# The first weight load of a decode block, split into 16 and 112 partitions, with other row distances in DRAM

## The chip, the cores and the metric

The kernel runs on one core of one Trainium2 chip. The metric is the time of one execution on the device, in microseconds. Several executions are timed, and their median counts. One execution more is recorded by the hardware profiler; the trace and the profile come from that one.

A core has these engines: PE multiplies matrices, DVE and ACT work on vectors, POOL is the general engine, and SP does nothing here but issue transfers. Sixteen DMA engines move the data between DRAM and the on-chip memory, which has 128 partitions. A transfer that SP or ACT issues is cut into packets, which the DMA engines take up.

## What is computed

One decode step of a transformer block, for eight sequences with one token each, all in float32. With `D = 1024`, 32 query heads, 4 key/value heads of width 128, the last 1,024 positions of the cache, and a hidden width of 3,584, the reference comes down to this:

```
q  = layernorm(x) @ wq                       # 1024 x 4096
p  = softmax(q . k_cache[last 1024] * 128**-0.5)
h  = x + (p . v_cache[last 1024]) @ wo       # 4096 x 1024
n  = layernorm(h)
out = h + (gelu(n @ w_gate) * (n @ w_up)) @ w_down   # 3584 wide
```

Every weight and every cache entry is read once and used for eight tokens only. That makes 111 MB to be loaded for one step.

## The kernel before, in words

The weights and the two caches are laid out on the host as twelve units of 128 rows by 16,384 elements, which is 65,536 bytes a row and 8 MiB a unit. In their order these are two units each for `wq`, the keys, the values and `wo`, and four for the gate and up projections with a part of the down projection. The last rows of the down projection follow in smaller arrays: `dn` (three loads), `tails` (two) and `ends` (two).

On the chip there are two buffers, `wbuf[0]` and `wbuf[1]` (L110, L111), for one unit each. Row p of a unit goes to partition p. The units alternate between the buffers, so that one is filled while PE works on the other.

The loop at L150 issues the twelve loads, all from SP and so on one queue, by way of the helper `move` (L91), which starts a transfer and lets it add 16 to a semaphore when it has landed. Unit 0 and unit 1 are issued at once. Each later unit waits until PE has finished with the unit two places before it (`free`, L152). The load of `x`, eight rows of 4,096 bytes to partitions 0, 4, ... 28, is issued from ACT behind the first unit (L155) and lies on a queue of its own.

DVE computes the layer norm of `x` (L247), PE turns the result by eight transposes (L240), and DVE copies it twice into the stationary operands `still[0]` and `still[1]` (`spread`, L271, the copy in L274). Each of these copies adds 1 to `go[0]` or `go[1]`. PE then runs passes of 64 multiplications over one buffer (`half`, L214, the multiplication in L222). Ahead of a pass it waits until that buffer's semaphore `go[i]` has 17: 16 from the load and 1 from the stationary operand (L232, L243). It takes the 17 off again, and so the same semaphore serves the next unit in that buffer.

After the first two passes come the scores, the softmax, the values, the output projection, the second layer norm and the gated projections in the same pattern. DVE and ACT prepare the next stationary operand while PE works on the other buffer. At the end the last rows of `down` are multiplied (L428, L454), added up (L457) and stored in two transfers, one from SP and one from ACT.

The function `kernel` (L484) prepares the arrays on the host. L517 joins the twelve units to one array, in which all rows lie back to back.

Of the kernel before, what the change touches and what calls it, by code (L numbers as in the profile page):

```python
# [7 lines left out]
P = 128  # L8
B = 8
D = 1024  # L10
# [4 lines left out]
NC = D // P  # L15
NQ = 4
# [3 lines left out]
BUF = NC * SET  # L20
# [10 lines left out]
ENDPARTS = (2, 1)  # L31
ENDS = (160, 96)
AHEAD = 3


GATE = (1, 16, 16)
# [5 lines left out]
class Flow:  # L42
# [37 lines left out]
    def run(self, engine, make, *waits, mark=True, gives=None):  # L80
        ins = self.start(engine, make, waits)
        if gives is not None:
            ins.then_inc(*gives)
            return None
        if not mark:
            return None
        self.done[engine] += 1
        ins.then_inc(self.own[engine], 1)
        return self.own[engine], self.done[engine]

    def move(self, name, out, src, *waits, engine="sync", sem=None):  # L91
        s = self.sem(name) if sem is None else sem
        self.start(engine, lambda e: e.dma_start(out, src), waits).then_inc(s, 16)  # L93
        return s, 16


def decode_block(nc, x, units, dn, tails, ends, outs):

    fl = Flow(nc)
    run, move = fl.run, fl.move  # L100
# [3 lines left out]
    def sb(name, *shape):  # L104
        return nc.alloc_sbuf_tensor(name, list(shape), F32).ap()
# [5 lines left out]
    wbuf = [space[:, i * BUF:(i + 1) * BUF] for i in range(2)]  # L111
# [6 lines left out]
    go = [fl.sem("go_a"), fl.sem("go_b")]  # L118
# [4 lines left out]
    at_mark = {}  # L123
# [26 lines left out]
    for u in range(UNITS):  # L150
        k, i = divmod(u, 2)
        free = None if k == 0 else (half_a, half_b)[i](k - 1)  # L152
        move(f"u{u}", wbuf[i], units[u], free, sem=go[i])
        if u == 0:
            x_in = move("x", x_sb[0:ROWS:STEP, :], x, x_zero, engine="scalar")  # L155

# [19 lines left out]
    for i, (n, src) in enumerate(zip(ENDS, ends)):  # L176
        t = wbuf[1][:, c0:c0 + NQ * n]
# [20 lines left out]
    own = sb("own", P, HB)  # L198
# [48 lines left out]
    def layernorm(src, ready, name, room):  # L247

        bn = sb(name + "_bn", ROWS, D // N, 6)
        tok = None  # L250
        for i in range(D // N):
            tok = run("vector", lambda e, i=i: e.bn_stats(bn[:, i], src[:, i * N:(i + 1) * N]), ready)
        mv, ve, sd, r0, r1, r2, rs = (
            sb(f"{name}_{n}", ROWS, k) for n, k in
            (("mv", 2), ("ve", 1), ("sd", 1), ("r0", 1), ("r1", 1), ("r2", 1), ("rs", 1))
        )
        tok = run("vector", lambda e: e.bn_aggr(mv, bn), tok)
        tok = run("vector", lambda e: e.tensor_scalar(ve, mv[:, 1:2], EPS, None, op0=ALU.add), tok)
        tok = run("scalar", lambda e: e.activation(sd, ve, AF.Sqrt), tok)
        tok = run("vector", lambda e: e.reciprocal(r0, sd), tok)  # L260

        tok = run("vector", lambda e: e.scalar_tensor_tensor(
            r1, r0, r0, ve, op0=ALU.mult, op1=ALU.mult), tok)
        tok = run("vector", lambda e: e.tensor_scalar(
            r2, r1, -0.5, 1.5, op0=ALU.mult, op1=ALU.add), tok)
        tok = run("vector", lambda e: e.tensor_mul(rs, r0, r2), tok)
        run("vector", lambda e: e.tensor_scalar(
            source[0:ROWS], src, mv[:, 0:1], rs, op0=ALU.subtract, op1=ALU.mult), tok, room,
            gives=(go_turn, 1))

    def spread(k):  # L271

        for i in range(2):
            run("vector", lambda e: e.tensor_copy(  # L274
                still[i].rearrange("p (c j m) -> p c j m", c=NC, j=NQ),
                turned.rearrange("p (c m) -> p c m", c=NC)[:, :, 0:32].unsqueeze(2).to_broadcast(
                    [P, NC, NQ, 32])), at_mark["t", k], gives=(go[i], 1))


    layernorm(x_sb, x_in, "ln1", src_ok)  # L280
    spread(0)


    side_by_side = [source[:, hf * N:(hf + 1) * N] for hf in range(2)]
# [12 lines left out]
    for hf in range(2):  # L297
# [3 lines left out]
        for s in range(2):  # L301
            for a in range(2):
                for b in range(HB):
# [6 lines left out]
                        gives=(go[hf], 1) if end else None)  # L310
# [3 lines left out]
    for hf in range(2):  # L314
# [7 lines left out]
        if hf == 1:  # L322
            run("vector", lambda e: e.tensor_copy(still[0], turned), at_mark["t", 2], half_a(1),
                gives=(go[0], 1))
# [4 lines left out]
        gives=(go[1], 1))  # L329


    for hf in range(2):
# [3 lines left out]
        for h in range(2):  # L336
            o3 = sums[hf][:, h * N:(h + 1) * N].rearrange("p (b d) -> p b d", b=HB)
            for b in range(HB):
# [5 lines left out]
                else:  # L344
# [3 lines left out]
                        gives=(go_turn, 1) if end and hf else None)  # L348
        cleared[hf] = run("gpsimd", lambda e: e.memset(still[hf], 0.0), done(2))  # L349

    for hf in range(2):
# [12 lines left out]
        gives=(go_fold, 1))  # L364
    h_sb = sb("h_sb", ROWS, D)
    h_ok = run("vector", lambda e: e.tensor_add(h_sb, x_sb, turned[0:ROWS]), at_mark["y", 3])
    layernorm(h_sb, h_ok, "ln2", None)
    run("gpsimd", lambda e: e.memset(note[:, 7:8], 0.0), at_mark["t", 5], gives=(go_fold, 2))
    spread(5)
    rest = sb("rest", P, N)  # L370
    for ch in range(2):
# [8 lines left out]
    for k, n in enumerate(SETS):  # L380
# [5 lines left out]
        if k == 1:  # L386
# [9 lines left out]
            gives=(go_turn, 1))  # L396
        t = turned[:, 0:N].rearrange("p (i m) -> p i m", m=P)
# [9 lines left out]
        else:  # L407
# [3 lines left out]
                at_ok, gives=(go_later[0], 1))  # L411
# [33 lines left out]

    ahead = sb("ahead", 1, AHEAD)
    for i in range(AHEAD):
        run("vector", lambda e: e.memset(ahead[:, i:i + 1], 0.0), arrived[last - 1][1], d1_ok)
# [110 lines left out]
```

## Time and profile before

| | |
|---|---|
| median of three runs | 263.96 us (263.74 to 263.99) |
| profiled execution | 263.65 us |
| its span, from the first to the last instruction | 262.3 us |
| mean granted clock of PE | 0.798 |
| PE, DVE, ACT, POOL busy | 140.4, 43.8, 13.5, 7.2 us |
| bytes read from DRAM | 111.18 MB |
| mean rate over the span | 424 GB/s |
| DMA packets | 3040 |

The profiled execution is timed like the others, and its span is the part between the first and the last instruction. In the views, "busy" is the time in which an engine worked on an instruction. Idle time is put down to what ended it, for example "<-PE sum L222" for a wait that ended with PE's multiplication into `sum` in line 222. The DMA rows give the share of the sixteen DMA engines' time that packets filled, and the rate in GB/s; a packet counts for the window in which it starts. For a transfer, the time to landing runs from its issue to the end of its last packet, and so it holds the time in the queue behind earlier transfers.

### The profile page before, as it was taken

Reading aid. Unit: us, or ns where it says so; the run is one execution under the profiler, and the core shown is the slowest. Engines: PE = TensorE matmul, PEld = TensorE weight load, DVE = VectorE, ACT = ScalarE, POOL = GpSimd, SP = SyncE. Lnnn points to the kernel's source line nnn. Section 1 sums busy time; section 2 is a strip of 40 time slices with the busy share of each in tenths; the row PEclk is TensorE's granted clock in tenths of the full one; section 3 lists DMA queues with packets and bytes.
Section 4 is the critical chain, followed back from the end, with each engine's and each line's share of the span. In section 5 each row is a group of like instructions: output and inputs, shape, how many; then the busy total and the mean of one; then the engine's idle time right before and its main releaser. Section 6 shows DMA issues by size and latency. Waiting matters only on the chain. (4 is left out here: it accounts for less than half of the span.)

```text
span 262.3 us, 2253 instructions
## 1 busy us (share of the span) xinstructions
PE 140.4 (54%) x968; PEld 44.4 (17%) x968; DVE 43.8 (17%) x115; ACT 13.5 (5%) x19; POOL 7.2 (3%) x18
## 2 busy tenths in 40 slices
PE   0025705926806937607918408728509709309985
PEld 0021201211202322102302102122102202002321
DVE  0340200240100140400410100254100300100332
ACT  1000000000030010000000200000300000200000
POOL 5000100100000000100100000000000000000000
PEclk9999975985966965975976956965977957956999
DMA  8998997999899799989979998997999999799896
GB/s 320 485 420 380 480 480 320 480 480 420 380 480 480 320 480 480 430 370 480 480 320 480 480 420 380 480 480 320 480 480 410 390 480 480 320 432 487 367 422 230
DMA packets 3040, 111.31 MB, mean 424 GB/s; under 512 B 472, under 2 KB 728, under 8 KB 992
## 3 DMA queue, kind: packets, MB, share of 16 engines
q1 hardware_dynamic: 2880, 111.23, 98.4%
q10 hardware_dynamic: 160, 0.08, 0.1%
HBM read 111.18 MB, written 0.13 MB: 424 GB/s over the span
## 5 line engine op out<-in xcount | busy, mean ns | idle before, releaser
L222 PE MATMUL sum<-w,still 128*32 128x512 f32 x832 | 116.1, 719 | 96.9 <-PEq L209 96.9
L222 PEld LDWEIGHTS sum<-w,still 128*32 128x32 f32 x832 | 31.9, 129 | 176.9 <-issue 176.9
L240 PE MATMUL turned<-ident,source 128*128 128x128 f32 x64 | 11.1, 331 | 21.0 <-PEq L209 21.0
L240 PEld LDWEIGHTS turned<-ident,source 128*128 128x128 f32 x64 | 8.9, 170 | 26.3 <-issue 26.3
L235 PE MATMUL turned<-y_sb,add 128*32 128x512 f32 x24 | 11.3, 592 | 0.9 <-PEq L209 0.9
L318 DVE TENSOR_REDUCE nmax<-sum 128x1 f32<-128x1024 f32 x2 | 2.5, 1225 | 28.4 <-PE sum L222 28.4
L393 DVE TENSOR_TENSOR up<-up,sum 128x512 f32<-128x512 f32 (+1 forms) x2 | 1.4, 686 | 34.2 <-PE sum L222 34.2
L289 DVE TENSOR_SCALAR q<-sum 128x512 f32<-128x512 f32 x2 | 1.4, 692 | 25.1 <-PE sum L222 25.1
L274 DVE COPY still<-turned 128x1024 f32<-128x1024 f32 x4 | 4.7, 1220 | 4.2 <-PE turned L240 4.2
L383 DVE TENSOR_TENSOR gate<-gate,sum 128x512 f32<-128x512 f32 (+1 forms) x2 | 1.4, 684 | 23.6 <-PE sum L222 23.6
L345 DVE SCALAR_TENSOR_TENSOR o<-sum,share,o 128x128 f32<-128x128 f32 x12 | 4.2, 351 | 4.2 <-PE sum L222 3.8
L342 DVE TENSOR_SCALAR o<-sum,share 128x128 f32<-128x128 f32 x2 | 0.7, 351 | 23.9 <-PE sum L222 23.9
L320 ACT ACT_TABLE_LOAD x1 | 1.3, 1283 | 60.1 <-DVE nmax L318 60.1
L235 PEld LDWEIGHTS turned<-y_sb,add 128*32 128x32 f32 x24 | 2.6, 110 | 8.7 <-issue 8.7
L349 POOL MEMSET still<- 128x1024 f32 x2 | 1.9, 952 | 76.0 <-PE sum L222 76.0
L362 DVE TENSOR_TENSOR y_sb<-y_sb,sum 128x512 f32<-128x512 f32 x1 | 0.7, 689 | 15.8 <-PE sum L222 15.8
L360 ACT COPY y_sb<-sum 128x512 f32<-128x512 f32 x1 | 0.6, 586 | 50.7 <-PE sum L222 50.7
L294 POOL MEMSET still<- 128x1024 f32 x2 | 1.9, 958 | 46.3 <-PE sum L222 46.3
L320 ACT ACTIVATE source<-sum,nmax 128x1024 f32<-128x1024 f32 x2 | 2.2, 1115 | 17.1 <-PE turned L240 17.1
L361 DVE TENSOR_TENSOR y_sb<-y_sb,sum 128x512 f32<-128x512 f32 x1 | 0.7, 689 | 14.3 <-PE sum L222 14.3
L305 DVE COPY still<-turned 128x16 f32<-128x16 f32 x32 | 2.7, 161 | 2.1 <-PE turned L240 2.1
L382 ACT COPY gate<-sum 128x512 f32<-128x512 f32 (+1 forms) x2 | 1.2, 584 | 30.3 <-PE sum L222 30.3
(61 smaller groups left out, 40.2 us busy)
## 6 DMA issues: line engine op xcount, KB each, us to landing
w<-dn SPq DMA_DIRECT2D x1, 5120.0 KB, 22.2
w<-dn SPq DMA_DIRECT2D x1, 2048.0 KB, 26.7
w<-dn SPq DMA_DIRECT2D x1, 1024.0 KB, 28.7
w<-tails SPq DMA_DIRECT2D x1, 1024.0 KB, 12.2
w<-tails SPq DMA_DIRECT2D x1, 512.0 KB, 13.1
w<-ends SPq DMA_DIRECT2D x1, 320.0 KB, 13.4
w<-units SPq DMA_DIRECT2D x12, 29.4
w<-ends SPq DMA_DIRECT2D x1, 192.0 KB, 13.4
```

What stands on the lines that cost most here:

```text
L222: ins = PE.matmul(sums[i][32 * j:32 * j + 32, h * N:(h + 1) * N], still[i][:, 32 * s:32 * s + 32], wbuf[i][:, s * N:(s + 1) * N], start=(c ...
L235: ins = PE.matmul(turned[0:32, ch * N:(ch + 1) * N], add2[:, ch, :], y_sb, start=True, stop=True)
L240: ins = PE.transpose(turned[:, n * P:(n + 1) * P], source[:, n * P:(n + 1) * P], ident)
L274: run("vector", lambda e: e.tensor_copy(still[i].rearrange("p (c j m) -> p c j m", c=NC, j=NQ), turned.rearrange("p (c m) -> p c m", c=NC) ...
L289: tok = run("vector", lambda e: e.tensor_scalar(q_sb, sums[hf][:, 0:N], scale, None, op0=ALU.mult), done(0, 0))
L294: cleared.append(run("gpsimd", lambda e: e.memset(still[hf], 0.0), done(0)))
L305: run("vector", lambda e: e.tensor_copy(to[:, :, b, s, a, REP * b:REP * b + REP].rearrange("p k (h i) -> p k h i", h=2), frm[:, s, a * HB ...
L318: tok = run("vector", lambda e: e.tensor_reduce(out=nmax, in_=sums[hf], axis=AX.X, op=ALU.max, negate=True), done(1))
L320: p_ok = run("scalar", lambda e: e.activation(source, sums[hf], AF.Exp, bias=nmax, accum_out=tot), tok, at_mark["t", 1 + hf])
L345: tok = run("vector", lambda e: e.scalar_tensor_tensor(out, o3[:, b], share[hf][:, b:b + 1], o_sb, op0=ALU.mult, op1=ALU.add), tok, done(2 ...
L349: cleared[hf] = run("gpsimd", lambda e: e.memset(still[hf], 0.0), done(2))
L383: tok = run("vector", lambda e: e.tensor_add(gate[:rows], gate[:rows], sums[0][:rows, N:2 * N]), tok, half_a(4 + k))
```

## The change

Three constants are added. `FIRST = 16` is the number of partitions of a new, separate first load. `GAP = 18880` elements, 75,520 bytes, is the distance of the rows of the second load. `PAD = 128` elements, 512 bytes, lie unused behind each row of the other eleven units.

The first unit is kept in two arrays of its own. `head` has rows 0 to 15, in rows of 7 x 18,880 elements, that is 528,640 bytes apart. `body` has rows 16 to 127, 75,520 bytes apart. Sixteen times seven rows of `body` begin at the same distances from one another as the sixteen rows of `head`. The rows of the other units are 66,048 bytes apart.

The load of unit 0 becomes two, issued one after the other from SP. The first fills partitions 0 to 15 and has a semaphore of its own, `first`. The second fills partitions 16 to 127 and adds to `go[0]` as before. So PE's wait for 17 covers the second load alone. The first is waited for by DVE: `spread(0, first)` puts the wait on the copies into the stationary operands, and without their increments PE does not start. What is computed, the order of the other loads and all multiplications stay.

```diff
+PAD = 128
+FIRST = 16
+GAP = 18880
...
-        move(f"u{u}", wbuf[i], units[u], free, sem=go[i])
+        if u == 0:
+            first = move("first", wbuf[i][0:FIRST], head[:, 0:BUF])
+            move("u0", wbuf[i][FIRST:P], body[:, 0:BUF], sem=go[i])
+        else:
+            move(f"u{u}", wbuf[i], units[u - 1][:, 0:BUF], free, sem=go[i])
...
-    def spread(k):
+    def spread(k, *waits):
 
         for i in range(2):
             run("vector", lambda e: e.tensor_copy(
                 still[i].rearrange("p (c j m) -> p c j m", c=NC, j=NQ),
                 turned.rearrange("p (c m) -> p c m", c=NC)[:, :, 0:32].unsqueeze(2).to_broadcast(
-                    [P, NC, NQ, 32])), at_mark["t", k], gives=(go[i], 1))
+                    [P, NC, NQ, 32])), at_mark["t", k], *waits, gives=(go[i], 1))
...
-    spread(0)
+    spread(0, first)
...
+    head = np.pad(units[0, 0:FIRST], ((0, 0), (0, (P // FIRST - 1) * GAP - BUF)))
+    body = np.pad(units[0, FIRST:P], ((0, 0), (0, GAP - BUF)))
+    units = np.pad(units[1:], ((0, 0), (0, 0), (0, PAD)))
```

More of the change, by code (lines that the diff above doesn't have):

```diff
@@ L94, in move, with decode_block @@
         return s, 16
-def decode_block(nc, x, units, dn, tails, ends, outs):
+def decode_block(nc, x, head, body, units, dn, tails, ends, outs):
     fl = Flow(nc)
@@ L531 @@
     arrays = {
-        "x": own(A_x).reshape(B, D), "units": own(units), "dn": dn, "tails": tails, "ends": ends,
+        "x": own(A_x).reshape(B, D), "head": own(head), "body": own(body), "units": own(units), "dn": dn, "tails": tails, "ends": ends,
     }
```

## The prediction

> **What bounds the kernel now.** I read the page first for its 40 slices and DMA queues, then the chain that ended last, the waits of the DMA-issuing queue, and last the DMA answers for short windows at the start.
>
> ```profile
> span 262.3 us, 2253 instructions
> ...
> PE 140.4 (54%) x968; PEld 44.4 (17%) x968; DVE 43.8 (17%) x115; ACT 13.5 (5%) x19; POOL 7.2 (3%) x18
> ...
> DMA  8998997999899799989979998997999999799896
> ...
> q1 hardware_dynamic: 2880, 111.23, 98.4%
> ```
>
> Queue q1 (SP's loads) carries 111.23 MB, and its packets fill 98.4% of the time of all sixteen DMA engines. The busiest compute engine, PE, is busy 54%. No slice of the DMA row stands at zero: the engines never run dry between the first load and the last.
>
> ```profile
> SPq L93 <- PE sum L222: 238.9, 12, 29.7
> ```
>
> ```profile
> w<-units SPq DMA_DIRECT2D x12, 29.4
> ```
>
> SP does wait for PE (238.9 us in 12 waits, for a buffer to come free), but that is no loss: a weight unit lands 29.4 us after its issue, and the next rows show that the transfer itself takes 19.4, so each load stands some 10 us in the queue behind its predecessor. Whatever makes the engines deliver earlier moves the whole program earlier; a PE step made shorter would not.
>
> ```profile
> core 0: us, PE busy (x) PEld busy (x) DVE busy (x) ACT busy (x) POOL busy (x), PEclk, DMA share, GB/s
> ...
> 100.00:119.36 19.36, 9.09 (x64) 2.50 (x64) 2.81 (x8) 0.00 (x0) 0.95 (x1) 0.76 1.00 433
> ```
>
> In the steady state 433 GB/s for 19.36 us are 8.4 MB, one unit of 128 rows of 65,536 bytes, at a DMA share of 1.00. Sixteen engines, eight rows each: 2.42 us a row, 27.1 GB/s an engine. PE needs 9.09 of these 19.36 us.
>
> ```profile
> DMA packets 16, 1.05 MB, mean 524 GB/s; under 512 B 0, under 2 KB 0, under 8 KB 0
> ...
> q1 hardware_dynamic: 16, 1.05, 152.9%
> ```
>
> ```profile
> DMA packets 16, 1.05 MB, mean 419 GB/s; under 512 B 0, under 2 KB 0, under 8 KB 0
> ...
> q1 hardware_dynamic: 16, 1.05, 96.7%
> ```
>
> These are the DMA answers for 1 to 3 us and for 4 to 6.5 us. A packet is credited to the window in which it starts, so a share can pass 100%. Each window holds exactly one row per engine. The first: 152.9% of 2 us on 16 engines is 48.9 us, 3.06 us a row. The second: 96.7% of 2.5 us on 16 engines is 38.7, 2.42 us a row. So every engine loses 0.64 us on its first row and, by the steady window above, nothing after it.
>
> ```profile
> 1.70:1.80 0.10, 0.00 (x0) 0.00 (x0) 0.00 (x0) 0.00 (x0) 0.10 (x1) 1.00 9.77 3277
> 1.80:2.00 0.20, 0.00 (x0) 0.00 (x0) 0.00 (x0) 0.00 (x0) 0.12 (x2) 1.00 5.90 1966
> 2.00:2.20 0.20, 0.00 (x0) 0.00 (x0) 0.00 (x0) 0.00 (x0) 0.20 (x2) 1.00 2.77 983
> 2.20:2.40 0.20, 0.00 (x0) 0.00 (x0) 0.18 (x1) 0.00 (x0) 0.20 (x1) 1.00 1.73 655
> ```
>
> ```profile
> 0.74 0.85 SPq L93 DMA_DIRECT2D w<-units  x2
> ```
>
> GB/s times width over 65,536 bytes gives how many engines start in each stretch: 5, 6, 3 and 2. The start is a ramp of some 0.6 us that begins 1.0 us after the issue at 0.74. The last two starters need 1.73 x 0.2 x 16 / 2 = 2.77 us for their row, less than the 3.06 of all.
>
> **The change part by part.** The sum is made against the profiled execution: 263.65 us, of which 262.3 are span and 1.35 lie around it. It stands 0.31 below the median of 263.96.
>
> *Row pitch and gaps in DRAM.* No byte more is read; the unused bytes are stepped over. In the steady state there is nothing to win on the rows shown, since the engines are full at 2.42 us a row with the present pitch of 65,536 bytes. Whether another pitch could lose is bounded by the first load of down-projection rows, 40,960 bytes long and apart, which fills this answer for 236 to 247 us:
>
> ```profile
> DMA packets 138, 4.80 MB, mean 436 GB/s; under 512 B 13, under 2 KB 13, under 8 KB 13
> ...
> q1 hardware_dynamic: 138, 4.80, 101.2%
> ```
>
> 436 GB/s at 101.2% is the same pace per engine. I take 0 for units 1 to 11. At the start, sixteen engines set out nearly together, at distances that are whole multiples of 65,536 bytes; if that is why they lose 0.64 us, the new distances cure it. Bounds: 0 (another cause) to -0.64 (all of it). I take -0.5, between the 0.29 that the last two starters already gain (3.06 - 2.77) and 0.64, nearer to the latter, since at 528,640 bytes no two of the sixteen are a multiple of 65,536 apart, while the last two starters still were.
>
> [...]
>
> *Two loads in place of one.* The first load now has one row per engine, the second seven. If the ramp is the time in which 128 rows are handed out, it shrinks to an eighth; if it is per engine, nothing changes. Bounds: 0 to -0.6 for the last starter. I take -0.3, half, because the mean engine starts only some 0.2 us behind the first. The seven remaining rows are issued one SP instruction later; such an instruction takes 328 to 426 ns here:
>
> ```profile
> L93 SPq DMA_DIRECT2D w<-units x12: 328/328/426, 0.7 to 205.4; - x12
> ```
>
> So they are issued by 1.2 us, and 1.0 to 1.6 us later (the row at 0.74 and the ramp) the engines have them: 2.2 to 2.8. The first rows are done at about 1.75 + 2.5 = 4.2. That cover is 1.4 us; were it gone, the engines would stand for what is missing. Unit 1 is issued 0.4 us later and needed at about 21: 0. One more completion per engine: a unit of 8 rows with its completion takes 19.36 against 8 x 2.42 = 19.36, below 0.02.
>
> *The added wait.* DVE's first expansion of the stationary operand (L274) also waits for `first`. Queued behind it on DVE is the second expansion, and PE's first multiplication waits for both:
>
> ```profile
> 16.15 2.36 DVE L274 COPY still<-turned 128x1024 f32<-128x1024 f32 x2 [2.12 <-PE turned L240]
> ```
>
> ```profile
> 22.68 8.54 PE L222 MATMUL sum<-w,still 128*32 128x512 f32 x64 [6.57 <-PEq L209]
> ```
>
> DVE comes to it at 16.15, some 12 us after `first` should be there, and PE starts at 22.68, 4.2 us after DVE's end at 18.51. Cost 0. If the weights come 0.8 earlier, 3.4 of that slack is left. Next in line after the start is again the DMA stream itself; the end is untouched.
>
> *Sum:* -0.5 - 0.3 = -0.8; 262.85 in the profile's terms, 263.2 as a median.
>
> **The rivals.**
>
> *Slower: neighbouring partitions share their way into the on-chip memory.* `first` sends all sixteen engines to partitions 0 to 15. If a way takes no more than one engine delivers, 27.1 GB/s, the steady window needs sixteen ways for a load over 128 partitions; at sixteen one way serves up to eight partitions, and sixteen neighbours have between two and sixteen ways: one to eight engines share one. With two sharing, the first row takes 2 x 2.42 = 4.84, 1.8 more than the 3.06 of now; with four 9.68, +6.6; with eight 19.4, +16.3. It decides from two engines on a way. I price it at the middle case, four: 263.96 + 6.6 = 270.6. The seven rows of the second load, if engine after engine takes seven neighbours, would meet in pairs now and then: 0 to 7 x 2.42 = 16.9 more. For it: no row of the trace has a bulk load on fewer than 128 partitions, so nothing shows that the ways are free to choose. Against it: nothing in the trace shows such sharing either.
>
> The Trainium skill ("SBUF — State Buffer", Door 1: The DMA port swizzle) states that partitions 0-15 reach four of sixteen ports and gives 104 GB/s measured there for 1 MiB. That is just the size of `first`: by that page an estimated 10.1 us for it, 7.0 more than now, and a time near 271. No run here shows it.
>
> *No change: a cold start.* The 0.64 us is what any first row costs, whatever its address, and the ramp belongs to the engines. Then the pitches do nothing and splitting at most 0.3: 263.7 to 264.0. For it: the second rows, started with the same spread of 0.6 us, lose nothing, though their distances are the same. Against it: the last two starters lose 0.35 where the mean loses 0.64, and a fixed price would be equal for all.
>
> *The rows are not dealt out evenly.* If 112 rows go to fourteen engines, eight each, these have nine rows in all: 2.42 - 0.8 = 1.6 more, 265.6. Against it: 112 divides by sixteen.
>
> **How the numbers follow.** Forecast 0.47, sharing 0.29, cold start 0.20, uneven 0.04. What a measurement of this kernel can tell from no change is about 0.2%, 0.53 us. The forecast's own range is 262.7 (263.96 - 0.64 - 0.6) to 263.6; a tenth of it lies within 0.53 of now. Faster: 0.43. Same: 0.20 and 0.04, 0.24. Slower: 0.29 and 0.04, 0.33. The range for 8 in 10 must take in part of the sharing: from 262.7 up to 273.5, that is +6.6 and about 3 us of pairing in the second load; beyond it are some 0.15, and below it 0.03.
>
> **What would show it.** Right: the answer for the first microseconds has sixteen packets of 65,536 bytes at about 2.5 us each, started within 0.1 to 0.2 us; unit 0 lands, and PE's first multiplication starts, 0.8 us earlier (about 21.9); the steady window still has 433 GB/s. Sharing: the first sixteen packets take 5 to 10 us each, and PE starts at 24 or later, at about 29 with four on a way. Cold start: 3.06 us a row again, PE at 22.4 or later. The forecast is wrong, too, if the pitch of the other units changes the steady 2.42 us a row, which would count 88 times per engine.

## The result, and the profile after

The changed kernel takes 285.45 us (median of 6 runs, 285.26 to 285.8) against 263.91 (263.74 to 264.04) for the kernel before: slower by 21.5 us, ratio 1.0819 with a 95% interval of 1.0808 to 1.0831. I had forecast 263.2 and a range up to 273.5. The likeliest case was wrong in sign, and the rival that has the right cause was priced too low.

The page of the changed kernel shows at once that the loss lies at the start:

```profile
span 283.9 us, 2255 instructions
...
DMA  9799799989999999999999989999999999989994
GB/s 148 148 300 268 175 277 415 425 388 415 443 443 443 443 425 443 443 443 443 443 434 434 425 379 425 434 443 443 443 434 434 443 443 443 443 389 415 410 411 184
...
q1 hardware_dynamic: 2896, 111.23, 98.2%
```

The DMA engines are as busy as before (98.2% after 98.4), and the bytes are the same. But "busy" here means that a packet is under way, not that it moves: in the first six slices, 43 us, the rate is 148 to 300 GB/s, and from then on it is about 430 GB/s, as before. A busy share without the rate beside it would have hidden the whole loss.

The next rows are the windows of the changed kernel, laid around the successive rows of unit 0; the row at 40.50 is the first of unit 1, and the last one a steady stretch. The last two columns are the share of the DMA engines and GB/s; wherever width times GB/s is 1.05 MB, there are sixteen rows in it, and share times width is the mean time of one.

```profile
core 0: us, PE busy (x) PEld busy (x) DVE busy (x) ACT busy (x) POOL busy (x), PEclk, DMA share, GB/s
1.50:3.50 2.00, 0.00 (x0) 0.00 (x0) 0.29 (x1) 0.56 (x1) 1.93 (x5) 1.00 4.23 524
8.50:11.50 3.00, 0.00 (x0) 0.00 (x0) 0.00 (x0) 0.00 (x0) 0.00 (x0) 1.00 1.80 350
15.25:17.25 2.00, 0.00 (x0) 0.00 (x0) 0.00 (x0) 0.00 (x0) 0.00 (x0) 1.00 2.41 537
19.50:21.50 2.00, 0.00 (x0) 0.00 (x0) 0.00 (x0) 0.00 (x0) 0.00 (x0) 1.00 1.69 524
23.40:25.70 2.30, 0.00 (x0) 0.00 (x0) 1.75 (x8) 0.20 (x1) 0.00 (x0) 1.00 1.65 456
27.00:30.00 3.00, 0.91 (x5) 0.51 (x3) 1.98 (x2) 0.00 (x0) 0.00 (x0) 1.00 1.53 350
31.50:34.50 3.00, 0.00 (x0) 0.00 (x0) 0.00 (x0) 0.00 (x0) 0.00 (x0) 1.00 1.58 350
36.00:39.00 3.00, 0.00 (x0) 0.00 (x0) 0.00 (x0) 0.00 (x0) 0.00 (x0) 1.00 1.50 350
40.50:43.50 3.00, 0.00 (x0) 0.00 (x0) 0.00 (x0) 0.00 (x0) 0.00 (x0) 1.00 1.10 350
...
60.00:79.36 19.36, 12.65 (x76) 3.93 (x76) 4.08 (x34) 0.00 (x0) 0.96 (x1) 0.75 1.00 433
```

The row of the first load takes 4.23 x 2 = 8.5 us where it took 3.06. The seven rows of the second take 5.4, 4.8, 3.4, 3.8, 4.6, 4.7 and 4.5 where each took 2.42. That is 39.7 against 3.06 + 7 x 2.42 = 20.0: 5.4 us lost in the first load, 14.3 in the second. The first row of unit 1 still takes 3.3 where it took 2.42. The engines also come out of it uneven. By the semaphore increments in the trace, the last engine lands unit 0 1.7 us after the mean engine, where it was 0.2. In the steady window, at 66,048 bytes from row to row, the rate is 433 GB/s as before.

The timeline of PE shows the sum, the start of the first multiplication:

```profile
25.97 1.94 PE L247 MATMUL turned<-ident,source 128*128 128x128 f32 x8 [25.97 <-PEq L216]
44.43 9.35 PE L229 MATMUL sum<-w,still 128*32 128x512 f32 x64 [16.52 <-PEq L216]
```

It starts at 44.43 where it was 22.68, 21.75 us later; the span is 21.6 longer. Of the 21.75, 19.7 are the rows of the mean engine and 1.5 the lag of the last one. The remaining 0.6 lie between an engine's last packet and its semaphore increment, 1.0 us in the mean where it was 0.4. After the first row of unit 1 nothing is lost and nothing is made good.

The layer norm of `x` comes late as well: by the packet records its eight rows start from 15.0 us on, where it was 7.1. That costs nothing, for DVE's copies into the stationary operands end at 30.38, 14 us before PE starts:

```profile
28.02 2.36 DVE L281 COPY still<-turned 128x1024 f32<-128x1024 f32 x2 [2.19 <-PE turned L247]
```

### The profile page after: what moved, and what is told of

It reads as the page before. It is cut to its first block, busy times and chain, and to the rows that moved or that the text cites. A ratio compares the mean times of both kernels' runs of the same rounds, so it can differ in the third digit from the quotient of the medians.

```text
span 283.9 us, 2255 instructions
## 1 busy us (share of the span) xinstructions
PE 144.0 (51%) x968; PEld 44.9 (16%) x968; DVE 43.8 (15%) x115; ACT 13.5 (5%) x19; POOL 7.2 (3%) x18
## 3 DMA queue, kind: packets, MB, share of 16 engines
q1 hardware_dynamic: 2896, 111.23, 98.2%
## 5 line engine op out<-in xcount | busy, mean ns | idle before, releaser
L229 PE MATMUL sum<-w,still 128*32 128x512 f32 x832 | 120.5, 742 | 103.2 <-PEq L216 103.2
L229 PEld LDWEIGHTS sum<-w,still 128*32 128x32 f32 x832 | 33.0, 133 | 186.3 <-issue 186.3
L247 PE MATMUL turned<-ident,source 128*128 128x128 f32 x64 | 10.4, 315 | 32.8 <-PEq L216 32.8
L247 PEld LDWEIGHTS turned<-ident,source 128*128 128x128 f32 x64 | 8.3, 161 | 38.1 <-issue 38.1
L242 PE MATMUL turned<-y_sb,add 128*32 128x512 f32 x24 | 11.3, 592 | 0.9 <-PEq L216 0.9
L259 DVE BATCH_NORM_STATS2 ln_bn<-x_sb 32x6 f32<-32x512 f32 x2 | 1.3, 672 | 19.7 <-DMA x_sb<-x 19.7
```

What stands on the lines that cost most here:

```text
L229: ins = PE.matmul(sums[i][32 * j:32 * j + 32, h * N:(h + 1) * N], still[i][:, 32 * s:32 * s + 32], wbuf[i][:, s * N:(s + 1) * N], start=(c ...
L242: ins = PE.matmul(turned[0:32, ch * N:(ch + 1) * N], add2[:, ch, :], y_sb, start=True, stop=True)
L247: ins = PE.transpose(turned[:, n * P:(n + 1) * P], source[:, n * P:(n + 1) * P], ident)
```

## The experiments

Theory 1: what counts is which partitions the sixteen engines write to at one time; partitions share ways into the on-chip memory, and engines on one way wait for each other. Theory 2: the new distances in DRAM. Theory 3: two loads on one queue hinder each other, whatever they fill. The diffs are shortened; `...` stands for lines that are not shown. Single runs are given with their time alone; the kernel before took 263.8 to 263.9 beside each of them.

### The split without the distances, and the distances without the split

`e1`, from the changed kernel:

```diff
-    head = np.pad(units[0, 0:FIRST], ((0, 0), (0, (P // FIRST - 1) * GAP - BUF)))
-    body = np.pad(units[0, FIRST:P], ((0, 0), (0, GAP - BUF)))
+    head = units[0, 0:FIRST]
+    body = units[0, FIRST:P]
```

Units 1 to 11 keep their 512 unused bytes.

> The split into 16 and 112 partitions stays, but unit 0 lies back to back in DRAM again (65,536 bytes from row to row in both loads). Theory 1 (sixteen engines that write to sixteen neighbouring partitions share the ways into the on-chip memory): the distances in DRAM play no part, the time stays within 2 us of 285.5, the first sixteen rows take 8 to 9 us each. Theory 2 (the new distances of 528,640 and 75,520 bytes slow the reads): the time returns to about 264, the first rows to about 3 us. Theory 3 (two loads on one queue hinder each other, wherever they go): about 285, but then experiments with more loads are slower by the number of loads.

Measured: 285.45 (285.04 to 285.86, 2 runs), ratio 1.0818 (1.0798 to 1.0838). The windows over its first three rows, by which they take 8.5, 5.5 and 4.9 us:

```profile
1.50:3.50 2.00, 0.00 (x0) 0.00 (x0) 0.29 (x1) 0.56 (x1) 1.93 (x5) 1.00 4.25 524
8.50:11.50 3.00, 0.00 (x0) 0.00 (x0) 0.00 (x0) 0.00 (x0) 0.00 (x0) 1.00 1.82 350
15.25:17.25 2.00, 0.00 (x0) 0.00 (x0) 0.00 (x0) 0.00 (x0) 0.00 (x0) 1.00 2.45 541
```

The changed kernel has 8.5, 5.4 and 4.8. Theory 2 falls for the loss: it stays when the new distances of unit 0 go.

`e2`, from the kernel before:

```diff
+PAD = 128
...
-        move(f"u{u}", wbuf[i], units[u], free, sem=go[i])
+        move(f"u{u}", wbuf[i], units[u][:, 0:BUF], free, sem=go[i])
...
+    units = np.pad(units, ((0, 0), (0, 0), (0, PAD)))
```

> One load for unit 0 as before; all twelve units get the 512 unused bytes behind each row. My forecast's term for the distances, alone: first rows 2.5 to 2.8 us in place of 3.06, time 0.3 to 0.5 below before (ratio 0.998). Cold start: first rows 3.06 again, ratio 1.000. Theory 2 in its wider form (any distance other than 65,536 slows the reads): slower by more than 1 us.

Measured: 263.74 (11 runs) against 263.84 (15), ratio 0.9996 (0.9987 to 1.0005). The DMA answer for 1 to 3 us of this kernel:

```profile
q1 hardware_dynamic: 16, 1.05, 151.8%
```

That is 3.04 us for the first row, where it was 3.06. No two rows of this unit lie a multiple of 65,536 bytes apart, and yet my forecast's term for the distances, -0.5, is not there. The exact distances of the change, 75,520 and 528,640 bytes, were not run with a load of all 128 partitions.

### Two loads that do not divide the partitions

`e7`, from the kernel before:

```diff
-        move(f"u{u}", wbuf[i], units[u], free, sem=go[i])
+        if u == 0:
+            cuts = [(slice(0, P), slice(0, 2048)), (slice(0, P), slice(2048, BUF))]
+            early = [move(f"first{n}", wbuf[i][c], units[u][c]) for n, c in enumerate(cuts[:-1])]
+            move("u0", wbuf[i][cuts[-1]], units[u][cuts[-1]], sem=go[i])
+        else:
+            move(f"u{u}", wbuf[i], units[u], free, sem=go[i])
...
-    spread(0)
+    spread(0, *early)
```

> Unit 0 as two loads that both go to all 128 partitions: the first 2,048 columns (8,192 bytes a row), then the other 14,336. Theory 1: no loss; the ramp term of my forecast (0 to -0.6) and whatever the first rows lose stay visible: 263.2 to 264.0. Theory 3 (two loads on one queue hinder each other wherever they go): about 285.

Measured: 263.77 (11 runs) against 263.87 (15), ratio 1.0 (0.9991 to 1.0009). Two loads cost nothing if both go to all partitions: theory 3 falls. They bring nothing either.

### Which partitions

The next five kernels use the same code, from the kernel before, with other `cuts` over the partitions of unit 0; the layout in DRAM stays as it was.

`e4`, eight loads of sixteen neighbours, `[slice(16 * r, 16 * r + 16) for r in range(8)]`:

> Unit 0 as eight loads of 16 neighbouring partitions each (0 to 15, 16 to 31, ...), layout in DRAM as before. Theory 1: every row of unit 0 takes 8.6 to 9.7 us, eight rows 69 to 77 in place of 20, time 313 to 321. Theory 2: about 264, since DRAM is laid out as before. Theory 3: as the eight loads with step 8, over 300; the two would not differ by much.

`e3`, every eighth partition, `[slice(r, P, 8) for r in range(8)]`:

> Unit 0 as eight loads of 16 partitions each, every eighth partition (0, 8, ... 120; then 1, 9, ...), layout in DRAM as before. Theory 1: sixteen partitions spread over all 128 reach more ways than sixteen neighbours; with twice as many ways a row takes about 4.6 us where neighbours took 8.6, eight rows some 37 in place of 20, time about 281; with all ways reached, 2.42 a row and about 264. Theory 2: the rows of one load are 524,288 bytes apart, which could be slow by itself, but there is no unusual gap: about 264. Theory 3: eight loads are worse than two: over 300.

`e8`, every fourth of one half, `[slice(h + r, h + 64, 4) for h in (0, 64) for r in range(4)]`:

> Unit 0 as eight loads of 16 partitions, every fourth of one half (0, 4, ... 60; 1, 5, ...; then 64, 68, ...). If four neighbouring partitions share a way and nothing else does, sixteen ways are reached: 2.42 us a row, about 264. If, as the port table of the Trainium skill has it, partitions 32 apart share one too, eight ways: 5.1 a row, about 285 as with step 8.

`e5`, halves, `[slice(0, 64), slice(64, 128)]`:

> Unit 0 as two loads of 64 partitions, 0 to 63 and 64 to 127. Theory 1 (what counts is which partitions the sixteen engines write to at one time): a load that reaches half of the ways lets two engines share one, as the loads with step 8 did: 5.1 us a row, eight rows 41 in place of 20, time about 285. Theory 3 (the loads hinder each other by their number): two loads, like the changed kernel, 285 as well. If half of the partitions have all the ways: 264.

Measured: 319.78, 285.14, 285.23 and 285.5. Here is the DMA answer of `e4` for 38 to 41 us, and a window of `e3`, of `e8` and of `e5`, each over one row of all sixteen engines:

```profile
q1 hardware_dynamic: 32, 1.05, 314.0%
```

```profile
16.00:18.50 2.50, 0.60 (x3) 0.63 (x4) 1.45 (x5) 0.06 (x1) 0.00 (x0) 1.00 2.05 419
```

```profile
16.90:18.90 2.00, 0.80 (x4) 0.83 (x5) 0.94 (x2) 0.00 (x0) 0.00 (x0) 1.00 2.56 524
```

```profile
17.00:19.00 2.00, 0.00 (x0) 0.00 (x0) 0.00 (x0) 0.00 (x0) 0.00 (x0) 1.00 2.56 524
```

They give 3.14 x 3 = 9.4 us a row for neighbours and 5.1 for the three others (I had expected 4.6 and a time of 281 for `e3`), about four times and twice the 2.42. `e4` and `e3` have eight loads each and differ by 34.6 us; two halves cost as much as eight loads with step 4. The number of loads does not explain that. The partitions do, or the rows in DRAM that go with them; the probes below tell these two apart. If it is the partitions, `e8` rules out that only neighbours share a way, since its sixteen are all four or more apart. It came out as expected if partitions 32 apart share one too; which partitions meet, no record names.

`e6`, sixteen neighbours and then seven loads with step 7, `[slice(0, 16)] + [slice(16 + r, P, 7) for r in range(7)]`:

> Partitions 0 to 15 as one load, then 16 to 127 as seven loads of 16 partitions with step 7 (16, 23, ... 121; then 17, 24, ...). If the changed kernel's second load gives engine e the seven neighbours from 16 + 7e on, this is the same order of writes, only in seven pieces: 283 to 287, later rows 3 to 5 us each. If that load is dealt out in another way, the rows with step 7 should meet less often: by the port table of the Trainium skill only two pairs of the sixteen meet at a time, rows of 2.4 to 4.8, unit 0 done about 31 us after the start, time about 275.

Measured: 285.8. Three windows of `e6` over its third, fourth and eighth row:

```profile
15.25:17.25 2.00, 0.00 (x0) 0.00 (x0) 0.00 (x0) 0.00 (x0) 0.00 (x0) 1.00 2.41 539
20.00:22.00 2.00, 0.60 (x3) 0.64 (x4) 1.09 (x3) 0.00 (x0) 0.00 (x0) 1.00 1.60 524
35.90:38.90 3.00, 0.00 (x0) 0.00 (x0) 0.00 (x0) 0.00 (x0) 0.00 (x0) 1.00 1.54 350
```

They take 4.8, 3.2 and 4.6 us, against 4.8, 3.4 and 4.5 for the same rows of the changed kernel, the fast one in the same place. So the load of 112 partitions behaves as if dealt out in neighbours, seven to an engine; the packet records name neither engine nor partition. If it were dealt out partition after partition, sixteen neighbours would meet at each step, at 9.4 us a row. But the estimate of 275 for rows with step 7 failed: with at most two pairs meeting at a time most engines should have taken 2.4 us a row, and five of the seven rows took about 4.5 or more in the mean. That called for a measurement of single sets.

### Single sets of sixteen partitions

`e10` and `e11`, from the kernel before, put probes ahead of the program. Each waits for the one before it, so that it has the queue to itself; only the last has unit 0 right behind it. The list of partitions, which differs between the two, is not shown:

```diff
+    prev = ()
+    for n, (to, frm) in enumerate(...):
+        half_row = BUF // 2
+        a = move(f"probe{n}a", wbuf[1][to, 0:half_row], units[1][frm, 0:half_row], *prev)
+        b = move(f"probe{n}b", wbuf[1][to, half_row:BUF], units[1][frm, half_row:BUF])
+        prev = (a, b)
...
-        move(f"u{u}", wbuf[i], units[u], free, sem=go[i])
+        move(f"u{u}", wbuf[i], units[u], free, *(prev if u == 1 else ()), sem=go[i])
```

> Ahead of the program, twelve probes, each alone on the queue, fill parts of the second buffer; each is two loads of the same partitions (half a row, 32,768 bytes, each: 1.21 us at full pace), and unit 1 is loaded over them afterwards. The program's own result is untouched; its time only grows by the probes. In order: 16 partitions from 32 on with step 4; from 11 with step 7; from 28 with step 4; from 24 with step 4; from 16 with step 7; from 0 with step 4; from 0 with step 8; 0 to 15; then 32 with step 4 again, read from rows 524,288 bytes apart, and from rows 65,536 apart; then partitions 16 to 127; then all 128. By the port table of the Trainium skill they reach 16, 16, 15, 14, 14, 8, 8, 4, 16 and 16 ways. Theory 1a (who shares a way pays, nobody else): second halves of 1.21 us with 16 ways; with 15, fourteen at 1.21 and two at 2.42; with 14, twelve and four; with 8 all 2.4 to 2.6; with 4 all 4.7. Theory 1b (sharing also holds back engines that share with nobody): 16 ways 1.21, but with 15 and 14 ways all rows grow, to 1.5 or more and to about 2.4. Theory 1c (an engine is fast only on its usual way): from 11 with step 7 slow, 2.4, although no two meet. Theory 2 (distances): the probe read from rows 524,288 apart slower than its twin.

The run took 384.4 us. These are the windows of `e10` over the second halves, in the order of the probes (16, 15, 14, 14, 8, 8, 4 and 16, 16 ways; the window of the first probe also holds packets of `x` and is left out):

```profile
9.00:11.00 2.00, 0.56 (x3) 0.59 (x4) 1.11 (x4) 0.00 (x0) 0.00 (x0) 1.00 0.61 262
14.50:16.50 2.00, 0.00 (x0) 0.00 (x0) 0.27 (x1) 0.00 (x0) 0.00 (x0) 1.00 0.70 262
22.00:24.00 2.00, 0.00 (x0) 0.00 (x0) 0.00 (x0) 0.00 (x0) 0.00 (x0) 1.00 1.31 262
28.80:30.80 2.00, 0.00 (x0) 0.00 (x0) 0.00 (x0) 0.00 (x0) 0.00 (x0) 1.00 1.22 262
36.00:38.00 2.00, 0.00 (x0) 0.00 (x0) 0.00 (x0) 0.00 (x0) 0.00 (x0) 1.00 1.29 262
43.00:45.00 2.00, 0.00 (x0) 0.00 (x0) 0.00 (x0) 0.00 (x0) 0.00 (x0) 1.00 1.28 262
51.00:55.00 4.00, 0.00 (x0) 0.00 (x0) 0.00 (x0) 0.00 (x0) 0.00 (x0) 1.00 1.21 131
62.00:64.00 2.00, 0.00 (x0) 0.00 (x0) 0.00 (x0) 0.00 (x0) 0.00 (x0) 1.00 0.61 262
67.00:69.00 2.00, 0.00 (x0) 0.00 (x0) 0.00 (x0) 0.00 (x0) 0.00 (x0) 1.00 0.62 262
```

Share times width, for half a row:

- Step 7 from 11, where no two meet: 1.22 us, the full pace. If the engines take the partitions in order, they are not on the ways of the 128-partition load here, and theory 1c falls; the records name no engine.
- One pair (28, step 4): mean 1.40. By the packet records, fourteen rows have 1.21 to 1.26 and two 2.55: only the pair pays, as theory 1a says.
- Two pairs (24, step 4, and 16, step 7): mean 2.62 and 2.44. Here all sixteen rows are slow, 2.58 to 2.60 in the first of them. Twelve engines that share with nobody lose as much as the four that do, as theory 1b says. So neither of the two theories holds whole.
- Eight ways: 2.58 and 2.56; four ways: 4.84.
- The same partitions filled from rows 524,288 bytes apart: 1.22; from sixteen neighbouring rows, 65,536 apart: 1.24. Theory 2 falls once more, and with it the rows in DRAM as the cause in `e3` and `e4`.

The last two probes load 112 partitions (16 to 127), and then all 128. These are the windows over seven of the fourteen half rows that each engine has in the first of them, over the other seven, and over most of the second:

```profile
70.50:84.00 13.50, 0.00 (x0) 0.00 (x0) 0.00 (x0) 0.00 (x0) 0.00 (x0) 1.00 1.08 272
84.50:99.00 14.50, 0.00 (x0) 0.00 (x0) 0.00 (x0) 0.00 (x0) 0.00 (x0) 1.00 1.00 253
105.50:122.50 17.00, 0.00 (x0) 0.00 (x0) 0.00 (x0) 0.00 (x0) 0.00 (x0) 1.00 1.00 432
```

With no other weight load beside it, the load of 112 partitions takes 2.1 us a half row and the load of 128 has its 432 GB/s. The second load of the change is slow by itself, whatever the first one does.

The Trainium skill ("SBUF — State Buffer", Door 1: The DMA port swizzle) gives the table of sixteen ports from which these numbers of ways are worked out. The runs agree with the table in every set tried. They are a little above its rate: 9.4 us for sixteen neighbours are 112 GB/s, where the page has 104 measured and about 109 as a limit. What the page does not give is the price of two pairs.

> Seven probes as in the probe kernel before, of 16 partitions each: from 36 with step 4 (one pair of engines on one way), from 40 with step 4 (two pairs), from 20 with step 4 (three pairs), from 18 with step 7 (one pair), from 12 with step 7 (two pairs), then from 24 with step 4 (two pairs) and from 28 with step 4 (one pair) again. If what was seen is a rule: with one pair two rows of 2.55 us and fourteen of 1.21; with two pairs or three all sixteen at 2.4 to 2.6. If it hung on the particular partitions or on the place in the order: one-pair probes with all rows slow, or two-pair probes with only four slow rows.

The run took 312.62 us. Windows of `e11` over the second halves of its second to sixth probe (two pairs, three pairs, one pair, two pairs, two pairs):

```profile
10.50:12.50 2.00, 0.80 (x4) 0.82 (x5) 0.94 (x2) 0.00 (x0) 0.00 (x0) 1.00 1.27 262
18.00:20.00 2.00, 0.00 (x0) 0.00 (x0) 0.00 (x0) 0.00 (x0) 0.00 (x0) 1.00 1.28 262
25.00:27.00 2.00, 0.00 (x0) 0.00 (x0) 0.00 (x0) 0.00 (x0) 0.00 (x0) 1.00 0.69 262
32.00:34.00 2.00, 0.00 (x0) 0.00 (x0) 0.00 (x0) 0.00 (x0) 0.00 (x0) 1.00 1.22 262
39.00:41.00 2.00, 0.00 (x0) 0.00 (x0) 0.00 (x0) 0.00 (x0) 0.00 (x0) 1.00 1.31 262
```

2.54, 2.56, 1.38, 2.44 and 2.62 us: one pair leaves the rest alone, two or three slow all sixteen. By the packet records the first and the last probe, one pair each, agree: fourteen rows of 1.21 to 1.28, and two of 2.5 in the first. In the last the two took 3.1 to 3.2, with unit 0 already behind them. The rule holds for other partitions and in another order, and so it is no accident of one set.

### A division that spares the ways

`e12`, with `[slice(32, 96), slice(0, 32), slice(96, 128)]`:

> Unit 0 as three loads: partitions 32 to 95, then 0 to 31, then 96 to 127. Dealt out in neighbours, the first gives engine e the partitions 32 + 4e to 35 + 4e and so all sixteen ways at each step; the two others give it two each, on eight ways. Theory 1: four rows at 2.42 and the usual start, then four at 5.1: 10.7 us more than before, 274.6. Theory 3 (the number of loads): as the halves or worse, 285 and more. Nothing but shared ways would make three loads cheaper than two.

Measured: 275.08, 11.3 us more than before where 10.7 were expected. Windows of `e12` over the second and the sixth row:

```profile
5.00:7.00 2.00, 0.00 (x0) 0.00 (x0) 0.00 (x0) 0.00 (x0) 0.00 (x0) 1.00 1.21 524
16.50:18.50 2.00, 0.02 (x1) 0.00 (x0) 0.00 (x0) 0.00 (x0) 0.00 (x0) 1.00 2.56 524
```

64 partitions from 32 to 95 load at the full 2.42 us a row, 64 from 0 to 63 (in `e5`) at 5.1. Three loads are 10 us faster than two. No version tried beats the kernel before by more than the interval.

## Why the prediction was wrong, point by point

**What bounds the kernel** was right: what the DMA engines lose in unit 0 is lost in the span (21.75 us at PE's first multiplication, 21.6 at the end), and the 10 us that each load waits in the queue did not absorb it. That wait is of the wrong kind for it: it covers a late buffer, not a slow engine.

**The step that failed** is "Two loads in place of one". I costed it by its issue, its ramp and its completions, at -0.3, and left out where its rows go. The change is one of partitions, and the effect of the partitions stood only among the rivals, with a chance of 0.29. The runs show +5.4 us for the first load and +14.3 for the second, because engines that write to partitions on one way hold each other up.

**The rival "sharing"** had the mechanism and its point of decision. Its first term was nearly right, four engines on a way: 9.68 us and +6.6 forecast, 8.5 and +5.4 measured. It stays below the 9.4 of the later rows of `e4`, probably because the engines start 0.7 us and end 2 us apart and so do not share all the time; no run isolates that. Its second term, "would meet in pairs now and then: 0 to 7 x 2.42 = 16.9 more", was left at 0 in the price of 270.6 and held to 3 in the range. Measured are 14.3, near the upper end. The reason is the rule of the probes: two pairs at a time are enough to slow all sixteen engines, and five of the seven steps of the second load have two pairs; the two with one pair are the rows with 3.4 and 3.8 us. These counts come from the port table of the Trainium skill ("SBUF — State Buffer", Door 1: The DMA port swizzle). The rule gives most of it, not all: five rows at twice 2.42 and two at 2.7 are an estimated 29.6 us, where 31.2 were measured. In the two rows with one pair the fourteen other engines took 3.0 to 3.7 us, not 2.42, and why is open; the engines are not at the same step at the same time there. I had written the bound down and then not let the range reach it.

**The weight against that rival** was "nothing in the trace shows such sharing either". The trace of before could not show it: every bulk load there fills all 128 partitions. Absence from such a trace is no evidence. The sentence from the Trainium skill beside it ("SBUF — State Buffer", Door 1: The DMA port swizzle) named the ports and 104 GB/s for just this size; it deserved more than the forecast.

**The distances**, -0.5: nothing, by `e2` and by the two twin probes, as far as they reach. What makes the first row slow is a start from idle. The probes show it again after each pause, with distances and partitions that are fast: here the first halves of the last two 16-way probes of `e10`.

```profile
60.00:62.00 2.00, 0.00 (x0) 0.00 (x0) 0.00 (x0) 0.00 (x0) 0.00 (x0) 1.00 0.91 262
65.50:67.50 2.00, 0.00 (x0) 0.00 (x0) 0.00 (x0) 0.00 (x0) 0.00 (x0) 1.00 0.85 262
```

1.82 and 1.70 us where the second halves took 1.22 and 1.24, 0.5 to 0.6 lost each time in the mean. The rival "cold start" was right on this term. My argument against it, that a fixed price would be equal for all starters, does not hold: by the packet records the rows of one such first half range from 1.2 to 2.1 us, and the first rows of the kernel before from 2.65 to 3.43. So it is also not every engine that loses 0.64 there; that is the mean.

**The ramp**, -0.3: nothing. With one row per engine in the first load, the sixteen start as they did with eight. Windows of the changed kernel:

```profile
1.70:1.80 0.10, 0.00 (x0) 0.00 (x0) 0.00 (x0) 0.00 (x0) 0.10 (x1) 1.00 25.34 3277
1.80:2.00 0.20, 0.00 (x0) 0.00 (x0) 0.00 (x0) 0.00 (x0) 0.12 (x2) 1.00 16.17 1966
2.00:2.20 0.20, 0.00 (x0) 0.00 (x0) 0.00 (x0) 0.00 (x0) 0.20 (x2) 1.00 8.26 983
2.20:2.50 0.30, 0.00 (x0) 0.00 (x0) 0.28 (x1) 0.00 (x0) 0.30 (x1) 1.00 3.47 437
```

5, 6, 3 and 2 starters, the very numbers of before. The ramp does not hang on the number of rows.

**The costs put at zero** hold. The units with 512 bytes of gap run at 433 GB/s. The added wait on DVE cost nothing: DVE comes to its copy at 28.02 us, and by the semaphore increments `first` had landed by 12.6. Nothing points to an uneven dealing to fourteen engines: the windows have sixteen rows at each step.

## What to carry to other kernels

When a load is divided, ask first which partitions its sixteen engines write to at each step, and only then what the issue, the gaps or the ramp cost; a division by columns leaves that alone, and every division of the unit by partitions tried here cost 11 us or more. The load of all 128 partitions ran at 2.42 us a row on all sixteen engines. By their row times, the loads of 64 and 112 partitions went out in runs of neighbours; of these, only the one of partitions 32 to 95 kept that pace. Two meetings at a time were enough to cost all sixteen engines half of it. Read the DMA share and the rate together: the DMA row stood at 9 tenths both in a slice with 148 GB/s and in one with 443.

## What the runs showed of the hardware

- Among sixteen partitions loaded alone, two engines on one way cost those two alone (2.4 to 2.55 us for half a row, the other fourteen 1.21). With a second pair, in every set tried, all sixteen came to 2.4 to 2.6. What couples them stays open. The Trainium skill ("DMA: Bandwidth & Descriptors", Back-pressure in remote DMA) says of transfers between cores that a saturated port clogs the path back to the engines that share it; no run here shows whether that is the cause.
- Sixteen engines that start from idle lose 0.5 to 0.64 us each, in the mean, on the first row: 0.64 with 65,536 bytes in the kernel before and 0.5 in `e12`, 0.5 to 0.6 with 32,768 bytes in `e10`.
- Rows 524,288 bytes apart in DRAM were read as fast as rows 65,536 apart, 1.22 and 1.24 us for half a row, into the same sixteen partitions (32, 36, ... 92).
